# Three attention visits with float32 weights transposed by TensorE and divided by GpSimd, and values loaded once per batch

## The chip, the cores and the metric

One core of a Trainium2 chip runs the kernel. The time is that of one execution in device microseconds; the text names the engines PE (TensorE; PEld its weight loads), DVE (VectorE), ACT (ScalarE), POOL (GpSimd) and SP (SyncE, which issues nearly all DMAs here).

## The reference: what is computed

Attention in which a query sees only the keys of its own hash bucket, for 4 batches, 8 heads, 768 positions and 64 elements per head, and behind it a feed-forward layer with two weight matrices (512 to 2048 and back) and a squared ReLU, which the code calls MoE:

```python
q_bits = (np.einsum('bhsd,dk->bhsk', q, proj) > 0).astype(np.int64)
mask = q_bucket[:, :, :, None] == k_bucket[:, :, None, :]
scores = np.where(mask, scale * np.matmul(q, k.transpose(0, 1, 3, 2)), -1000000000.0)
attn = np.exp(scores - np.max(scores, axis=-1, keepdims=True))
attn = attn / (np.sum(attn, axis=-1, keepdims=True) + 1e-09)
x = np.matmul(attn, v).transpose(0, 2, 1, 3).reshape(B * S, H * D)
h = np.maximum(x @ w_in, 0.0)
return (h * h @ w_out).astype(np.float32)
```

All is float32, and the kernel keeps nearly that accuracy on fp16 matmuls: a number is split into an fp16 `hi` and an fp16 `lo` (what is left), and a product is made of three: hi by hi, hi by lo, lo by hi.

## The kernel before

**Visits and units.** The work is cut into visits: a batch, a pair of heads, and a half of the 768 queries (384). There are 32, and the first six are the pairs 0 and 1 of batch 0 with both halves, then pair 2 and pair 3 with half 0. A visit has six units (two heads by three blocks of 128 queries), so there are 192. One unit (`unit`, L651 to L673) does this:

- PE: scores `pS` of 128 queries by 768 keys; the mask is folded into the operands. In the first eight visits (batch 0) these are float32 matmuls over 128 rows, of which the trace shows two passes each; later ones are in a float32 form that takes less.
- DVE: `nmx`, the negated maximum of a row, read from PSUM.
- ACT: `e`, the exponential, with the row's sum `sm` beside it.
- POOL or DVE: `rv`, the sum scaled; DVE: its reciprocal.
- ACT (seldom POOL or DVE): the hi half `hl[:, 0] = e * rv` in fp16; DVE: the lo half, one instruction that reads `e` and the hi half.
- SP: one DMA transpose of both halves into `aT` (128 x 12 x 128, fp16).

When the six units of a visit have their `aT`, `av` (L679 to L686) multiplies them by the values: 36 matmuls in 18 pairs, the two heads of a pair side by side in the array, into `pA`. ACT and DVE split that again into `xx`.

**Values.** For each batch `scale_values` (L619) loads all four pairs of v, squares them (ACT), sums the squares of each row (DVE, `rows`) and takes the maximum, from which the power of two comes that v is scaled with. `values` (L638) then loads each pair once more and splits it into `VV`.

**MoE.** When the four pairs of a half are there, a stage of the MoE can start, of 112 steps with three matmuls each: `pm` (by w_in), ReLU and square and split on ACT and DVE (`g`), and `po` (by w_out). There are eight stages; the first needs the visits 0, 2, 4 and 5. During the first visits w_in and w_out are loaded too (`raw`, `f`) and split into fp16 halves (`win`, `wo`); at the end of the first stage `wo` is rescaled (`align`).

**Order.** The functions only record operations. A planner (`order`, `forward`, `backward`) then places them on the engines by estimated durations, ready times and ranks, and where an operation may run on several engines (`move`, `square`) it also chooses the engine. `emit` writes the result out; each engine takes its instructions in this order. A rule ties the MoE's steps to the units (`PACE`): step 0 not ahead of unit 25, step 120 not ahead of unit 64. And `emit` puts fillers in front of PE's instructions where the planner sees PE idle: matmuls of a tile of ones, without use for the result, into the PSUM tile with the tag `pm`, and only up to the first operation that needs a `pm` tile (`busy_from`):

```python
for i in out[: out.index(self.busy_from)]:
    ...
        if o.start > end + 300:
            fill[i] = int((o.start - end) * IDLE_SHARE / 56)
```

Line numbers: everything that is recorded comes out at L402, pairs and fours of matmuls at L399, fillers at L395; so the profile is read by tiles, not by lines. PSUM's eight banks are the tags `pS` (2), `po` (3, also used for the scores of every second unit up to unit 36), `pm`, `pA` and `misc` (1 each).

Of the kernel before, what the change touches and what calls it, by code (L numbers as in the profile page):

```python
# [40 lines left out]
ROUNDS, BEHIND = 4, 40000  # L41

PREP, STACKS, VALUES = -9, 0, 2
WIN_RANK, WOUT_RANK = (18, 2.0), (30, 2.5)
RANK_PE, RANK_MOE = 1e6, -1.0

PLAIN, ALTERNATE = 4, 36

WHOLE = {0: 2}
# [14 lines left out]

SWITCH = 95

# [46 lines left out]
class Program:  # L113
# [60 lines left out]
    def cost(key, name, args, kw):  # L174
# [10 lines left out]
        n = max(size(args[0]), size(args[1]) if isinstance(args[1], View) else 0)  # L185
        if key == "pe":
            t = max(107, size(args[2]) * column.get(args[2].dtype, 1 / 2.4) + 3)
            return t, t
        if name.startswith("dma"):
            b = int(np.prod(args[0].shape)) * mybir.dt.size(args[0].dtype)  # L190
            inside = name == "dma_start_transpose" or kinds[:2] == ["sb", "sb"]
            busy = 1040 if key == "pool" else (650 if inside else 475) + 50 * (key == "act")
            return busy, b / (175 if name == "dma_start_transpose" else 314)
        if key == "act":
# [9 lines left out]
    @staticmethod  # L204
    def tiling(o):

        _, w, x = (o.args[0][0] if o.name == "matmuls" else o.args)[:3]
        size = lambda n: min(m for m in (32, 64, 128) if n <= m)
        return size(w.shape[0]), 128 if w.dtype == F32R else size(int(np.prod(w.shape[1:])))

# [84 lines left out]
    def forward(self, prio, near):  # L295
# [20 lines left out]
        while True:  # L316
# [37 lines left out]
            if k == "pe":  # L354
                last, kind = kind, self.tiling(o)
                if last != kind:
                    busy, done = busy + SWITCH, done + SWITCH
            o.start, o.busy = t, busy
            if o.name.startswith("dma"):
# [55 lines left out]
def lsh_attention_moe(ctx: ExitStack, tc, kq, v, proj2, w_in, w_out, consts, out):  # L415
# [195 lines left out]

    vscales = {}

    def load(b, hp):
        RV = sb([P, 2, KC, D], F32, "RV")
        send(RV, v[b, hp])
        return RV

    def scale_values(b):  # L619

        tops = sb([P, H // 2], F32, "vtop", 2)
# [16 lines left out]
    def values(b, hp):  # L638
# [11 lines left out]

    def unit(st, half, i, aT):  # L651
        c0 = half * HS + i * P
# [14 lines left out]
        rv = sb([P, 1], F32, "rv", 3)  # L667
        pr.add(*[(q, "tensor_scalar", (rv, sm, 1e-9, 1.0 / ASC, ALU.add, ALU.mult), {}) for q in (dve, pool)])
        dve.reciprocal(rv, rv)
        hl = sb([P, 2, S], F16, "hl", BUFS["hl"])  # L670
        move(hl[:, 0], e, rv)
# [7 lines left out]
    def av(b, hp, half, VV, aTs):  # L679
        pA = ps([P, 512], F32, "pA")[:, 0:HS]  # L680
        todo = [(kc, t * D, kc + l * KC) for t, l in ((0, 0), (1, 0), (0, 1)) for kc in range(KC)]
        for n, (kc, d0, c) in enumerate(todo):
            matmuls(*[(pA[m], VV[:, h, kc, d0 : d0 + D], aTs[h][:, c]) for h, m in enumerate((T, U))], start=n == 0, stop=n == len(todo) - 1)
        xx = xxs[b, half, hp] = sb([P, 2, HS], F16, "xx")
        move(xx[:, 0], pA, 1.0 / ASC)
        left(xx[:, 1], pA, 1.0 / ASC, xx[:, 0])  # L686

# [115 lines left out]
    for n, (b, hp, half) in enumerate(visits):  # L803
        sts, aTs = kept[b, hp], []
        for h, st in enumerate(sts):
            aT = sb([P, 2 * KC, HS], F16, "aT", BUFS["aT"])
            aTs.append(aT)
            for i in range(3):
                pr.rank = u
                unit(st, half, i, aT)  # L810
# [3 lines left out]
        if (b, hp) not in kept_v or not alive([kept_v[b, hp]]):  # L814
            pr.rank = u - 6 + PREP
            kept_v[b, hp] = values(b, hp)
        pr.rank = u - 0.5
        av(b, hp, half, kept_v[b, hp], aTs)
        if n in early:
# [41 lines left out]
```

## Time and profile before

| | |
|---|---|
| median of 3 runs | 924.09 us (924.06 to 924.19) |
| the profiled execution | 925.36 us, its span 923.6 us |
| PE busy | 885.6 us (96%) |
| DVE busy | 643.8 us (70%) |
| ACT busy | 663.6 us (72%) |
| POOL busy | 54.8 us (6%) |
| DMA | 149.99 MB, mean 162 GB/s |

A row of a group reads: line, engine, operation, output tile <- input tiles, shapes, count | busy us in all, mean ns of one | idle us of the engine just before them, and what ended it. A row of a window: the stretch, its length, busy time (and count) of each engine, the clock that PE was granted (1.00 is full), the DMA engines' busy share, GB/s. A row of a timeline: start, duration, engine, operation, count, and the idle time before it. Records of one engine overlap a little, so that the distance of two starts is what an instruction holds of its engine.

### The profile page before, as it was taken

The numbers are of one execution on the slowest core, as the hardware profiler recorded it, in microseconds if no ns is written. First come the engines' busy times: TensorE is split into PE (matmuls) and PEld (weight loads), VectorE is DVE, ScalarE is ACT, GpSimd is POOL, SyncE is SP. The second block draws the span as 40 slices with busy tenths as digits, with TensorE's granted clock in tenths as the row PEclk, the third lists the DMA queues.
The fourth block names the chain that finished last, engine by engine and source line by source line (L and its number), as shares of the span: only waits on it lengthen the run. The fifth ranks groups of instructions, "written<-read, shape, count | busy, mean of one in ns | idle before, by whom it ended". The sixth has DMA issues, their size and how long they took to land.

```text
span 923.6 us, 15264 instructions
## 1 busy us (share of the span) xinstructions
PE 885.6 (96%) x5592; PEld 501.3 (54%) x5592; DVE 643.8 (70%) x1206; ACT 663.6 (72%) x1166; POOL 54.8 (6%) x104
## 2 busy tenths in 40 slices
PE   7988988999997999999999999999999999999997
PEld 6555555445554555555555556555555555554553
DVE  5999999988979687889686768797867651211111
ACT  4877987878879677888777768787778673533433
POOL 0111301200103000000000000000000000000000
PEclk9999999999999999999999999999999999999999
DMA  7998999997999797999697959897878640200000
GB/s 236 248 222 210 226 237 213 250 211 193 236 203 242 133 192 148 185 234 244 145 198 159 190 121 198 174 213 154 170 149 177 121 102 10 77 1 0 35 1 35
DMA packets 329323, 149.99 MB, mean 162 GB/s; under 512 B 305568, under 2 KB 305696, under 8 KB 329248
## 3 DMA queue, kind: packets, MB, share of 16 engines
q1 hardware_dynamic: 329248, 149.02, 73.6%
q8 instruction: 44, 0.72, 0.3%
q14 instruction: 31, 0.25, 0.1%
HBM read 43.59 MB, written 6.29 MB: 54 GB/s over the span
## 4 chain that ended last, share of the span: by engine, by line
PE 63%; ACT 5%; DMA 2%; DVE 2%; issue 1%; POOL 0%; SPq 0%; ACTq 0%; DVEq 0%
PE po L402 23%; PE pm L402 21%; PE pS L402 9%; PE pA L399 8%; ACT wo L402 1%; DMA aT<-hl 1%; ACT e L402 1%; PE pd L399 1%; DMA RV<-vp 1%; ACT hl L402 1%; DVE hl L402 1%; ACT g L402 1%; PE pc L402 1%; DVE nmx L402 1%; DMA M<-Q 1%
## 5 line engine op out<-in xcount | busy, mean ns | idle before, releaser
L402 PE MATMUL po<-wo,g 128*128 128x512 f16 x1152 | 332.7, 381 | 2.7 <-ACT wo L402 0.9
L402 PE MATMUL pm<-xx,win 128*128 128x384 f16 x1536 | 322.4, 327 | 1.3 <-DVE g L402 1.0
L402 DVE TENSOR_REDUCE nmx<-pS 128x1 f32<-128x768 f32 x192 | 183.1, 954 | 57.7 <-PE pS L402 56.6
L402 ACT ACTIVATE e<-pS,nmx 128x768 f32<-128x768 f32 x192 | 171.6, 894 | 67.8 <-DVE nmx L402 48.8
L402 DVE SCALAR_TENSOR_TENSOR hl<-e,rv,hl 128x768 f16<-128x768 f32 x192 | 194.1, 1012 | 26.1 <-ACT hl L402 25.5
L402 PEld LDWEIGHTS <-win 128*128 128x128 f16 x1536 | 145.1, 98 | 115.4 <-issue 17.8
L402 ACT ACTIVATE hl<-e,rv 128x768 f16<-128x768 f32 x188 | 173.5, 928 | 25.1 <-ACT e L402 14.0
L402 PEld LDWEIGHTS <-g 128*128 128x128 f16 x1152 | 107.9, 98 | 131.3 <-issue 26.4
L402 DVE SCALAR_TENSOR_TENSOR g<-g,g 128x384 f16<-128x384 f32 x122 | 67.5, 554 | 127.7 <-ACT g L402 127.1
L402 ACT ACTIVATE g<-pm 128x384 f32<-128x384 f32 x125 | 60.7, 486 | 108.3 <-PE pm L402 107.4
L402 ACT ACTIVATE g<-g 128x384 f32<-128x384 f32 (+1 forms) x248 | 128.8, 520 | 10.8 <-PE po L402 5.6
L399 PE MATMUL pA<-aT,VV 128*64 128x384 f16 x1152 | 117.8, 331 | 0.0
L402 PE MATMUL pS<-A,Q 128*128 128x384 f32 x288 | 95.2, 411 | 5.0 <-ACT e L402 4.8
L399 PEld LDWEIGHTS <-VV 128*64 128x64 f16 x1152 | 59.5, 109 | 55.8 <-issue 35.8
L402 PE MATMUL pS<-L,M 128*128 128x384 f32 x288 | 77.8, 350 | 0.2
L402 PEld LDWEIGHTS pS<-A,Q 128*128 128x128 f32 x288 | 49.3, 190 | 29.8 <-ACT e L402 15.9
L402 POOL TENSOR_SCALAR rv<-sm 128x1 f32<-128x1 f32 x74 | 28.8, 389 | 610.6 <-ACT e L402 604.0
L395 PEld LDWEIGHTS <-ones 128*128 128x128 bf16 x756 | 49.9, 103 | 20.1 <-issue 11.8
L395 PE MATMUL idle<-ones 128*128 128x128 bf16 x756 | 54.7, 228 | 2.7 <-DVE ones L402 2.7
L402 PEld LDWEIGHTS pS<-L,M 128*128 128x128 f32 x288 | 51.9, 189 | 3.9 <-issue 2.4
L402 PE MATMUL pS<-Q,M 128*128 128x384 f32 x96 | 37.3, 510 | 9.5 <-ACT e L402 9.1
L402 PE MATMUL pS<-A,L 128*128 128x384 f32 x96 | 36.6, 508 | 5.7 <-ACT e L402 5.4
(92 smaller groups left out, 579.9 us busy)
## 6 DMA issues: line engine op xcount, KB each, us to landing
RV<-vp SPq DMA_DIRECT2D x32, 384.0 KB
R<-kq SPq DMA_DIRECT2D x24, 384.0 KB
raw<-w_in SPq DMA_DIRECT2D x16, 511.8 KB
raw<-w_out SPq DMA_DIRECT2D x16, 511.8 KB
out<-o SPq DMA_DIRECT2D x21, 256.0 KB
Q<-L SPq DMA_DIRECT2D x24, 192.0 KB
Q<-A SPq DMA_DIRECT2D x24, 192.0 KB
L<-M SPq DMA_DIRECT2D x24, 192.0 KB
```

The costliest lines, as they stand in the source:

```text
L395: issue(q, q.engine.matmul(self.idle[0].real(), self.idle[1].real(), self.idle[1].real(), start=True, stop=True).ins)
L399: ins = q.engine.matmul(*map(real, args), **kw).ins
L402: ins = getattr(q.engine, o.name)(*map(real, o.args), **{k: real(x) for k, x in o.kw.items()}).ins
```

## The change

Three of the first five visits (`PLAIN_AV`: 0, 2 and 4, all of batch 0, 18 units) get another path from `e` to `aT`. POOL alone divides: it multiplies `e` by `rv` in place, in float32. PE transposes each of the six 128 x 128 blocks, three into a bank with the tag `pm` and three into one with the tag `pA`. ACT or DVE copies each of the two banks into `aT`, which is float32 in these visits. `hl` and the DMA transpose go. The values of these visits are the loaded float32 tile, unscaled, so `av` has 12 matmuls, in 6 pairs, instead of 36; the scale of v comes in when `pA` is split.

Values: the tile loaded for the scale is kept and used for the split (or, in the plain visits, as it is); 16 loads instead of 32. The square is one ACT instruction that writes the sum too; DVE's `rows` and `vtop` go. `unit_f`, the identity, gets a buffer of its own, and `VV` has six buffers, which v shares.

The planner's prices change a little (lines of `SWITCH`, `TRANSPOSES`), and with the operations everything is placed anew. The fillers end ahead of the first transpose now, since that is the first that needs a `pm` tile (`pr.busy_from` in `unit`).

```diff
-BUFS = dict(xx=12, hl=3, raw=2, f=7, e=3, aT=3, g=2, A=2, Q=2, L=2, M=2, RV=2, VV=4)
+BUFS = dict(xx=12, hl=3, raw=2, f=7, e=3, aT=3, g=2, A=2, Q=2, L=2, M=2, RV=2, VV=6)
...
+PLAIN_AV, DIVIDE = (0, 2, 4), ("pool",)
...
-SWITCH = 95
+SWITCH, ENTRY = 95, 105
+TRANSPOSES = 165
...
-    unit_f = sb([P, P], F32, "unit_f", tag="o")
+    unit_f = sb([P, P], F32, "unit_f")
...
         for hp in range(H // 2):
-            RV = load(b, hp)
-            rows = sb([P, 2 * KC], F32, "rows", 2)
-            square(RV, RV)
-            dve.tensor_reduce(rows, RV.rearrange("p h c d -> p (h c) d"), AX.X, ALU.add)
-            dve.tensor_reduce(tops[:, hp : hp + 1], rows, AX.X, ALU.max)
+            pr.rank = r0 + LOADS * hp
+            RV = loaded[b, hp] = sb([P, 2, KC, D], F32, "V", tag="VV")
+            send(RV, v[b, hp])
+            act.activation(sb([P, 2, KC, D], BF16, "sqv"), RV, AF.Square, accum_out=tops[:, hp : hp + 1])
...
-        RV = load(b, hp)
+        if plain:
+            return loaded[b, hp]
+        RV = loaded.pop((b, hp))
         VV = sb([P, 2, KC, 2 * D], F16, "VV")
...
+        if plain:
+            move(e, e, rv, tuple(getattr(pr, k) for k in DIVIDE))
+            for g in range(2):
+                pT = ps([P, 512], F32, "pT", tag=("pm", "pA")[g])[:, 0:HS]
+                pr.busy_from = min(pr.busy_from, len(pr.ops))
+                for c in range(3):
+                    kc = 3 * g + c
+                    pe.matmul(pT[:, c * P : (c + 1) * P], e[:, kc * P : (kc + 1) * P], unit_f, start=True, stop=True, is_transpose=True)
+                move(aT[:, 3 * g : 3 * g + 3, i * P : (i + 1) * P], pT.rearrange("p (c s) -> p c s", c=3), 1.0, (act, dve))
+            return
...
-        todo = [(kc, t * D, kc + l * KC) for t, l in ((0, 0), (1, 0), (0, 1)) for kc in range(KC)]
+        plain = VV.dtype == F32
+        todo = [(kc, t * D, kc + l * KC) for t, l in (((0, 0),) if plain else ((0, 0), (1, 0), (0, 1))) for kc in range(KC)]
+        scale = vscales[b][0] if plain else 1.0 / ASC
...
-            aT = sb([P, 2 * KC, HS], F16, "aT", BUFS["aT"])
+            aT = sb([P, KC, HS], F32, "aT") if plain else sb([P, 2 * KC, HS], F16, "aT")
```

How it moves the instructions is seen at three places. First DVE in the first units, from the second pair of score maxima on (`rv` is the reciprocal chain, `f` and `top` belong to w_in, `tov` and `norm` to the scale of v). Before:

```order
L402 TENSOR_REDUCE nmx<-pS 128x1
L402 SCALAR_TENSOR_TENSOR hl<-e,rv,hl 128x768
L402 TENSOR_SCALAR top_73<-raw 128x512
L402 SCALAR_TENSOR_TENSOR hl<-e,rv,hl 128x768
L402 SCALAR_TENSOR_TENSOR f<-raw,top_73 128x512
L402 TENSOR_REDUCE nmx<-pS_358 128x1
L402 RECIPROCAL rv<-rv 128x1
```

And now:

```order
L410 TENSOR_REDUCE nmx<-pS 128x1
L410 RECIPROCAL rv<-rv 128x1
L410 SCALAR_TENSOR_TENSOR f<-raw,top_79 128x512
L410 TENSOR_REDUCE norm<-pt 128x1
L410 TENSOR_REDUCE nmx<-pS_329 128x1
L410 TENSOR_SCALAR rv<-sm 128x1
```

The two hl between a maximum and the next are gone. Up to the sixth visit's xx DVE has 41 hl before and 22 now, 4 `rows` and none, 26 conversions to win and wo and 22, 43 maxima and 42, and one copy `aT<-pT`; ACT has 41 hl before and 22 now, and 35 copies `aT<-pT`.

Second PE at the same place (`pt<-dg,ones` belongs to the scale of v). Before, with fillers of L395 on both sides:

```order
L395 MATMUL idle<-ones 128x128
L402 MATMUL pS<-A,L 128x384 x2
L402 MATMUL pS_358<-Q,M 128x384 x2
L402 LDWEIGHTS ones
L402 MATMUL pt<-dg,ones 128x128
L395 LDWEIGHTS ones
```

And now:

```order
L410 MATMUL pS<-A,L 128x384 x2
L410 MATMUL pT<-unit_f,e 128x128 x3
L410 MATMUL pS_329<-Q,M 128x384
L410 LDWEIGHTS ones
L410 MATMUL pt<-dg,ones 128x128
L410 MATMUL pS_329<-Q,M 128x384
L410 MATMUL pT<-unit_f,e 128x128 x3
```

The transposes stand between the scores of later units, and no filler comes behind the first of them: 756 fillers before, 130 now. Ahead of the first `pm` PE has 88 score matmuls before and 86 now.

Third SP at the start (`cst`, `pj`, `sgn_f` and `unit_f` are constants; `A`, `Q`, `R` hold k and q). Before:

```order
L402 DMA Q<-kq 128x768
L402 DMA RV<-vp 128x768 x2
L402 DMA cst<-consts 128x4
L402 DMA pj<-proj 128x6 x2
L402 DMA sgn_f<-consts 6x64 x8
L402 DMA raw<-w_in 128x2047
L402 DMA R<-kq 64x768
```

And now:

```order
L410 DMA pj<-proj 128x6 x2
L410 DMA Q<-kq 128x768
L410 DMA sgn_f<-consts 6x64 x8
L410 DMA cst<-consts 128x4
L410 DMA R<-kq 64x768
L410 DMA V<-vp 128x768 x2
L410 DMA raw<-w_in 128x2047
```

The constants and the first R stand ahead of v now. Over the whole kernel SP has 192 transposes before and 174 now, and 32 loads of v and 16.

More of the change, by code (lines that the diff above doesn't have):

```diff
@@ L41 @@
 ROUNDS, BEHIND = 4, 40000
+LOADS = 0
 PREP, STACKS, VALUES = -9, 0, 2
@@ L186, in cost @@
         if key == "pe":
+            if "is_transpose" in kw:
+                return 110, 110
             t = max(107, size(args[2]) * column.get(args[2].dtype, 1 / 2.4) + 3)
@@ L192, in cost @@
             busy = 1040 if key == "pool" else (650 if inside else 475) + 50 * (key == "act")
-            return busy, b / (175 if name == "dma_start_transpose" else 314)
+            return busy, b / (TRANSPOSES if name == "dma_start_transpose" else 314)
         if key == "act":
@@ L355, in forward @@
                 last, kind = kind, self.tiling(o)
-                if last != kind:
+                if last is None or last[:2] != kind[:2]:
                     busy, done = busy + SWITCH, done + SWITCH
+                elif kind[2] and not last[2]:
+                    busy, done = busy + ENTRY, done + ENTRY
             o.start, o.busy = t, busy
@@ L610, in prep @@
         return out
[L612 to L617, printed above, removed]
+    vscales, loaded = {}, {}
     def scale_values(b):
+        r0 = pr.rank
         tops = sb([P, H // 2], F32, "vtop", 2)
         for hp in range(H // 2):
-            RV = load(b, hp)
-            rows = sb([P, 2 * KC], F32, "rows", 2)
-            square(RV, RV)
-            dve.tensor_reduce(rows, RV.rearrange("p h c d -> p (h c) d"), AX.X, ALU.add)
-            dve.tensor_reduce(tops[:, hp : hp + 1], rows, AX.X, ALU.max)
+            pr.rank = r0 + LOADS * hp
+            RV = loaded[b, hp] = sb([P, 2, KC, D], F32, "V", tag="VV")
+            send(RV, v[b, hp])
+            act.activation(sb([P, 2, KC, D], BF16, "sqv"), RV, AF.Square, accum_out=tops[:, hp : hp + 1])
         top = sb([P, 1], F32, "top")
@@ L636, in scale_values, with values @@
         vscales[b] = scales(norm, "v", 4)
-    def values(b, hp):
+        pr.rank = r0
+    def values(b, hp, plain):
         r0 = pr.rank
@@ L648, in values, with unit @@
         return VV
-    def unit(st, half, i, aT):
+    def unit(st, half, i, aT, plain):
         c0 = half * HS + i * P
@@ L667, in unit @@
         rv = sb([P, 1], F32, "rv", 3)
-        pr.add(*[(q, "tensor_scalar", (rv, sm, 1e-9, 1.0 / ASC, ALU.add, ALU.mult), {}) for q in (dve, pool)])
+        pr.add(*[(q, "tensor_scalar", (rv, sm, 1e-9, 1.0 if plain else 1.0 / ASC, ALU.add, ALU.mult), {}) for q in (dve, pool)])
         dve.reciprocal(rv, rv)
+        if plain:
[8 more added lines that the diff above has]
+            return
         hl = sb([P, 2, S], F16, "hl", BUFS["hl"])
@@ L684, in av @@
         xx = xxs[b, half, hp] = sb([P, 2, HS], F16, "xx")
-        move(xx[:, 0], pA, 1.0 / ASC)
-        left(xx[:, 1], pA, 1.0 / ASC, xx[:, 0])
+        move(xx[:, 0], pA, scale)
+        left(xx[:, 1], pA, scale, xx[:, 0])
     def unscaled(b, j=None):
@@ L803, in lsh_attention_moe @@
     for n, (b, hp, half) in enumerate(visits):
-        sts, aTs = kept[b, hp], []
+        sts, aTs, plain = kept[b, hp], [], n in PLAIN_AV
         for h, st in enumerate(sts):
-            aT = sb([P, 2 * KC, HS], F16, "aT", BUFS["aT"])
+            aT = sb([P, KC, HS], F32, "aT") if plain else sb([P, 2 * KC, HS], F16, "aT")
             aTs.append(aT)
@@ L809, in lsh_attention_moe @@
                 pr.rank = u
-                unit(st, half, i, aT)
+                unit(st, half, i, aT, plain)
                 u += 1
@@ L813, in lsh_attention_moe @@
             ready(*visits[n + 1][:2], u + PREP, visits[n + 1][0] == 0 and visits[n + 1][1] < PLAIN)
-        if (b, hp) not in kept_v or not alive([kept_v[b, hp]]):
+        if (b, hp, plain) not in kept_v or not alive([kept_v[b, hp, plain]]):
             pr.rank = u - 6 + PREP
-            kept_v[b, hp] = values(b, hp)
+            kept_v[b, hp, plain] = values(b, hp, plain)
         pr.rank = u - 0.5
-        av(b, hp, half, kept_v[b, hp], aTs)
+        av(b, hp, half, kept_v[b, hp, plain], aTs)
         if n in early:
```

2 lines of the change are left out of this document (1 added, 1 removed).

## The prediction

> **What bounds the kernel now.** I read the windows of busy time first, split where the profile changes character; the columns are PE, PEld, DVE, ACT and POOL busy, the granted clock, DMA share and GB/s.
>
> ```profile
> 0.00:20.00 20.00, 14.62 (x143) 12.46 (x144) 9.14 (x20) 7.68 (x10) 0.20 (x4) 0.91 0.74 220
> 20.00:170.00 150.00, 132.51 (x1087) 83.02 (x1086) 143.70 (x287) 120.77 (x202) 24.64 (x43) 1.00 1.01 228
> 170.00:200.00 30.00, 28.39 (x160) 14.32 (x159) 29.15 (x58) 27.03 (x49) 4.05 (x6) 1.00 0.98 231
> 200.00:272.00 72.00, 70.72 (x434) 39.48 (x433) 61.38 (x119) 58.69 (x105) 5.22 (x12) 1.00 0.96 217
> 272.00:298.00 26.00, 21.32 (x130) 12.24 (x129) 25.48 (x47) 25.09 (x33) 8.81 (x12) 1.00 0.98 223
> 298.00:924.00 626.00, 618.02 (x3646) 339.83 (x3644) 375.01 (x680) 424.32 (x770) 11.84 (x27) 1.00 0.63 133
> ```
>
> From 298 us on PE is busy 618 of 626 us: the end is PE's. Before 170 us it looks busy as well (132.5 of 150), but the groups of that stretch say with what:
>
> ```profile
> L395 PE MATMUL idle<-ones 128*128 128x128 bf16 x631 | 42.9, 219 | 0.0
> L402 DVE TENSOR_REDUCE nmx<-pS 128x1 f32<-128x768 f32 x44 | 41.8, 952 | 2.3 <-PE pS L402 2.2
> L402 DVE SCALAR_TENSOR_TENSOR hl<-e,rv,hl 128x768 f16<-128x768 f32 x41 | 41.5, 1011 | 0.8 <-ACT hl L402 0.8
> L402 ACT ACTIVATE e<-pS,nmx 128x768 f32<-128x768 f32 x43 | 38.4, 894 | 21.7 <-DVE hl L402 9.7 <-DVE nmx L402 5.5 <-DVE rv L402 4.5
> L402 ACT ACTIVATE hl<-e,rv 128x768 f16<-128x768 f32 x41 | 37.4, 925 | 0.1
> L402 PE MATMUL pS<-Q,M 128*128 128x384 f32 x84 | 32.8, 511 | 9.0 <-ACT e L402 8.6
> L399 PE MATMUL pA<-aT,VV 128*64 128x384 f16 x216 | 19.8, 329 | 0.0
> ```
>
> 42.9 us of it are filler matmuls that nobody reads, so PE does 89.6 us of work in 150. DVE is busy 143.7 (96%) and hardly ever waits (2.3 us for scores, 0.8 for hl), DMA's share is 1.01, ACT has 120.8 (81%). So two things are full at once: DVE by its own instructions, DMA by its transposes and loads. The stretch ends with the first matmul of the MoE:
>
> ```profile
> 169.50 1.30 PE L402 MATMUL pm<-xx,win 128*128 128x384 f16 x7
> ```
>
> From there PE has real work to put into every gap: of the 754 us that are left it is busy 738.4 (the sum of the last four windows), and some 15 us are lost. So the time is 169.5 us up to the first MoE matmul (T1 below), plus 754 us that are PE's. The change touches units of the visits 0, 2 and 4, all ahead of T1. What it is worth is how much earlier T1 comes, less what is given back behind it.
>
> **The change part by part.** Counts are from the orders of the two kernels, taken on each engine up to the sixth visit's xx, which is what the first MoE matmul waits for.
>
> *DVE.* Of hl's second halves 41 stand there before and 22 after: 18 belong to the plain units, one has moved behind T1. What one holds of the engine is the distance of starts:
>
> ```profile
> 106.65 1.01 DVE L402 SCALAR_TENSOR_TENSOR hl<-e,rv,hl 128x768 f16<-128x768 f32 x1
> 107.58 0.95 DVE L402 TENSOR_REDUCE nmx<-pS 128x1 f32<-128x768 f32 x1
> 108.44 0.15 DVE L402 RECIPROCAL rv<-rv 128x1 f32<-128x1 f32 x1
> ```
>
> 0.93 us each, so 18 x 0.93 = 16.7 us gone. The sums of squares of v go too (four `rows` of batch 0 and their maxima), but two of the four stood ahead of 19 us, where DVE was idle half the time; the other two at 0.95 count, 2 us with their small maxima. Only one of the 36 copies of transposed weights falls to DVE, +0.5. Net 18.2 us. Besides, five conversions of w_in (three at 0.69, two shorter), a score maximum and that hl stand behind T1 now, about 4.9 us. DVE ahead of T1: 143.7 - 23.1 = 120.6 us.
>
> ```profile
> L402 DVE TENSOR_REDUCE rows<-RV 128x12 f32<-128x768 f32 x16 | 15.0, 945 | 6.7 <-ACT RV L402 6.6
> L402 DVE TENSOR_SCALAR g<-pm 128x384 f32<-128x384 f32 x3 | 1.7, 553 | 0.2 <-PE pm L402 0.2
> L402 ACT ACTIVATE xx<-pA 128x384 f16<-128x384 f32 x31 | 15.0, 483 | 16.1 <-PE pA L399 15.7
> L402 POOL TENSOR_SCALAR hl<-e,rv 128x768 f16<-128x768 f32 x3 | 2.9, 954 | 0.6 <-DVE rv L402 0.6
> L402 DVE SCALAR_TENSOR_TENSOR f<-raw,top 128x512 uint32<-128x512 uint32 x27 | 18.7, 697 | 0.0
> L402 DVE SCALAR_TENSOR_TENSOR win<-f,towin,win 128x512 f16<-128x512 f32 x16 | 12.0, 770 | 0.8 <-POOL win L402 0.8
> L402 POOL TENSOR_SCALAR rv<-sm 128x1 f32<-128x1 f32 x30 | 11.7, 389 | 113.0 <-ACT e L402 109.7 <-DVE hl L402 3.4
> ```
>
> *ACT* trades 19 hl at 0.925 (17.6 us) for 35 copies out of PSUM, nearest row xx<-pA at 0.483 (16.9 us); the squares of v keep their place and gain an accumulator read each. It comes out even: 121 us.
>
> *POOL* gets 18 divisions of 128x768; the nearest row is its three hl at 0.954, so 17 us, on an engine with 24.6 of 150 busy. Its own time is free, but it disturbs: its 128x1 scaling takes 0.389 us in the mean, most of it behind DVE's long instructions with two inputs from SBUF (hl, f, win). If such a pair excludes each other, each division that meets one holds DVE back by half its length. Those instructions fill about 60 of DVE's 121 us (22 hl and 4 of v at 0.93, 26 f at 0.70, 22 of the weights at 0.77 or less); 18 x 0.5 x 0.48 = 4 us. Bounds: 0 (DVE goes first always) and 17.
>
> *PE* loses the fillers, and three visits of 36 fp16 matmuls in pairs (19.8 / 2 = 9.9 us); it gets 36 float32 ones in pairs, each in two passes as pS has them, and 108 transposes.
>
> ```profile
> 26.38 1.56 PE L402 MATMUL pS<-Q,M 128*128 128x384 f32 x4 [0.23 <-ACT e L402]
> 27.77 1.11 PE L395 MATMUL idle<-ones 128*128 128x128 bf16 x17
> ```
>
> Four float32 passes over 384 columns take 1.56 us, 0.39 each, so a pair of value matmuls is 0.78 and three visits 18 x 0.78 = 14 us. No float32 transpose is in this trace. Below lies the filler, 128 columns at 1.11 / 17 = 0.065 us (7 us in all), above two passes of a pS at 0.39 / 3 each beside a weight load of 0.19 (41 us in all); I take one pass of 128 float32 columns, 0.13, 14 us. PE's work is 89.6 - 9.9 + 14 + 14 = 108 us, 101 to 135.
>
> The Trainium skill (VectorE: DVE Perf Modes, section on the three transpose paths) gives 390 ns for a 128x128 bf16 transpose on TensorE. By that figure, as an estimate, the transposes would be 42 us and PE's work 136. No run here shows it yet.
>
> *DMA* loses 18 transposes of the 36 of this stretch and four loads of v; its share was 1.01, so it drops out as a bound. And its order at the start changes: the small constants stand ahead of v now. Before, DVE's cast of the signs stood idle 2.9 us for a load:
>
> ```profile
> 12.86 0.43 DVE L402 CAST sgn<-sgn_f 128x512 bf16<-128x512 f32 x1 [2.89 <-DMA raw<-w_in]
> 18.30 2.80 PE L402 MATMUL pS<-A,L 128*128 128x384 f32 x8
> ```
>
> I let the first scores come 3 us earlier (0 to 4).
>
> *T1.* With the start at 17 instead of 20: DVE needs (120.6 + 4) / 0.96 = 130 us, the 0.96 being what it reached before. ACT needs 121 us of its own; the most that it reached before T1 in any 20 us was 18.31:
>
> ```profile
> 40.00:60.00 20.00, 18.08 (x137) 11.12 (x135) 19.90 (x39) 18.31 (x32) 3.19 (x9) 1.00 0.97 218
> ```
>
> At 0.92 that is 131 us. PE's 108 us fit in. So T1 = 17 + 131 = 148 us, 21.5 earlier, with DVE and ACT as bounds side by side.
>
> *Behind T1.* The 4.9 us of DVE work that has moved lands in a stretch like 170 to 200, where DVE is full (29.15 of 30): I give back half, 2.5 us. In 272 to 298, where PE loses 4.7 us, ACT rescales w_out:
>
> ```profile
> L402 ACT ACTIVATE wo<-wo,rel 128x1024 f16<-128x1024 f16 x15 | 16.2, 1138 | 0.0
> L402 DVE TENSOR_SCALAR wo<-wo,rel 128x1024 f16<-128x1024 f16 x1 | 0.5, 466 | 0.0
> ```
>
> The order has 9 of these on ACT now, 6 on DVE and 1 on POOL: I count 2 us of the 4.7 as won. The loads and squares of v in the batches 1 to 3 go in a stretch that is PE's: nothing.
>
> *The clock.* Without fillers PE has gaps. The rows (PE alone: busy, clock, DMA) of the two places in the trace where that happened:
>
> ```profile
> 9.00:12.00 3.00, 1.84 (x25) 1.00 0.54 131
> 12.00:15.00 3.00, 1.50 (x18) 0.94 0.99 287
> 15.00:18.00 3.00, 3.00 (x27) 0.50 1.01 283
> 18.00:21.00 3.00, 3.00 (x17) 0.99 1.05 378
> ...
> 294.00:298.00 4.00, 2.08 (x11) 1.00 1.02 219
> 298.00:302.00 4.00, 4.00 (x13) 0.58 1.06 271
> ```
>
> A stretch with PE half idle costs half the clock for the three or four us behind it; 61% busy did not yet. At 108 of 131 us (82%) I expect a few such dips, like the one in 272 to 302: about 4% of PE's work, 4 us, of which 3 on the path.
>
> Sum: -21.5 + 2.5 - 2 + 3 = -18 us. The profiled execution took 925.36 us (span 923.6), the median of the runs is 924.09, 1.3 less; the difference is carried over to the median: 906.1 us.
>
> **The rivals.**
>
> 1. *The hand-offs eat it.* A plain unit goes ACT e, reciprocal, POOL, PE, ACT, each engine taking its instructions in order, with three buffers for e and one bank for each half of pT. For it: ACT's idle time ahead of e is 21.7 us already, all behind DVE. Against it: ACT, the receiver, has other work in between. If each of 18 units holds ACT up by 0.5 us more, 9 us: 915.
>
> 2. *More than I count.* ACT and DVE both wait less when DMA is no longer full: ACT at 0.97 makes T1 142, and all of the 4.7 us behind are won; without clock loss that is -27.5 - 4.7 + 2.5, near -30: 894. Against it: ACT has never run so full ahead of T1.
>
> 3. *Slower, by the clock.* If the granted clock stays down through the stretch, PE is the bound: from 17 us on it has 108 us to do, and at a mean clock c takes 108 / c. Even with before is c = 108 / 152.5 = 0.71; at 0.6 T1 comes at 197, 27.5 us late: 952. For it: the fillers go, and 0.50 and 0.58 stand in the rows above. Against it: those dips end after some 3 us of work, and a PE that falls behind is busy, which brought 0.99 each time. The Trainium skill (TensorE: Matmul & The Clock Gate, Part 4 on the PE-mode transpose) says that transposes do not count as busy for the clock gate as matmuls do. By that rule 94 of 131 us count instead of 108, 72%, still over the 61% that kept the clock here; it gets 6% from me.
>
> 4. *Nothing comes of it*, because the MoE's steps are tied to units and w_in's last chunks come later: 924. DVE's total work up to 298 us falls by about 20 us whatever the order, so this gets 2%.
>
> **How the numbers follow.** The forecast has 0.62, with ends at 897 and 915: port 0 instead of 4, start 4 and all of the 4.7 below; POOL's upper bound or a transpose at its upper end above (PE at 135 of 131 us makes T1 155 or so). Rival 1 has 0.20, rival 2 has 0.10, rival 3 0.06, rival 4 0.02. 893 to 919 leaves out rival 3 and 4 and some of the tails. What can be told from no change here is 0.2%, 1.8 us: faster 0.92, same 0.02, slower 0.06.
>
> **What would show it.** In the profile after: the first pm at 144 to 152 us; DVE and ACT both above 90% between 20 us and there; DMA's share at 0.8; no filler behind the first transpose; POOL's division near 0.95; the transposes' distance near 0.13; the clock mostly at 1.00 with dips. A first pm at 160 with ACT waiting for pT says rival 1; a clock of 0.7 or less over the stretch says rival 3. An early T1 with an end that has not moved would make the forecast wrong where I trust it most: that behind T1 the time is PE's.

## The result, and the profile after

The kernel after takes 914.86 us (median of 4 runs, 912.07 to 916.78), the kernel before 924.14 beside it (4 runs): a ratio of 0.988, interval 0.9847 to 0.9913. So it is faster, by 9.3 us where the forecast had 18. The profiled execution took 913.5 us with a span of 911.7; before it was 925.36 and 923.6. A second measurement is the first experiment below; it gave 11.3 us. In three of the sets below (the loading of v alone, a price of 175, the two that helped together) one run took 1261 to 2259 us; the ratios leave it out, and the medians change by at most 0.15 us with it.

The windows of the kernel after, cut at its own first MoE matmul (153.5 us) and then as before:

```profile
0.00:20.00 20.00, 15.28 (x142) 11.66 (x143) 7.37 (x16) 8.60 (x14) 0.20 (x4) 0.92 0.74 231
20.00:153.50 133.50, 112.09 (x525) 56.77 (x524) 121.62 (x253) 115.25 (x216) 43.06 (x62) 0.95 0.79 192
153.50:200.00 46.50, 44.99 (x261) 23.48 (x260) 41.66 (x84) 42.51 (x79) 7.79 (x11) 1.00 1.02 218
...
272.00:298.00 26.00, 25.48 (x147) 13.88 (x148) 19.09 (x34) 21.17 (x38) 0.33 (x1) 1.00 1.05 200
298.00:912.00 614.00, 604.01 (x3558) 328.04 (x3556) 360.91 (x650) 413.21 (x754) 17.75 (x31) 1.00 0.65 128
```

Ahead of T1 DMA's share is 0.79 instead of 1.01, POOL has 43 us instead of 24.6, and DVE is busy 91% where it was 96%. In 272 to 298, where w_out is rescaled, PE is busy 25.48 us instead of 21.32.

The groups between 20 us and T1:

```profile
L410 DVE TENSOR_REDUCE nmx<-pS 128x1 f32<-128x768 f32 x41 | 38.9, 952 | 9.0 <-PE pS L410 8.8
L410 ACT ACTIVATE e<-pS,nmx 128x768 f32<-128x768 f32 x42 | 38.1, 909 | 7.2 <-DVE nmx L410 4.7 <-DVE rv L410 1.7 <-POOL rv L410 0.3
L410 PE MATMUL pS<-A,L 128*128 128x384 f32 x80 | 33.8, 545 | 7.3 <-ACT e L410 4.5 <-ACT L L410 2.8
L410 PE MATMUL pS<-Q,M 128*128 128x384 f32 x84 | 33.7, 519 | 7.8 <-ACT e L410 7.7
L410 DVE SCALAR_TENSOR_TENSOR hl<-e,rv,hl 128x768 f16<-128x768 f32 x22 | 22.4, 1019 | 0.2
L410 POOL TENSOR_SCALAR e<-e,rv 128x768 f32<-128x768 f32 x18 | 18.8, 1048 | 38.3 <-DVE rv L410 28.5 <-PE pS L410 3.3 <-PE pc L410 2.3
L410 PE MATMUL pT<-unit_f,e 128*128 128x128 f32 x108 | 17.2, 277 | 1.8 <-ACT aT L410 1.2 <-POOL e L410 0.6
L410 ACT ACTIVATE aT<-pT 128x384 f32<-128x384 f32 x35 | 16.5, 502 | 1.1 <-PE pT L410 0.9
L407 PE MATMUL pA<-aT,V 128*64 128x384 f32 x72 | 12.9, 494 | 0.0
```

Of hl on DVE 22 are left, POOL divides 18 times, ACT copies 35 times: the counts of the order. What is new is in the last column: DVE waits 9.0 us for scores (2.3 before). ACT waits 7.2 us ahead of its exponential, 21.7 before. The scores wait 12.2 us for that exponential (7.7 and 4.5); this is not new, since before it was 13.7 (8.6 for `Q,M`, and 5.1 in this row of the stretch from 20 to 170 us), with fillers in a part of the gaps:

```profile
L402 PE MATMUL pS<-A,L 128*128 128x384 f32 x88 | 33.7, 508 | 5.4 <-ACT e L402 5.1 <-ACT L L402 0.3
```

The timeline of PE, at the first scores, at six transposes in a row, at the first float32 value matmuls, and at T1:

```profile
15.52 2.96 PE L410 MATMUL pS<-A,L 128*128 128x384 f32 x6 [2.07 <-ACT L L410]
...
25.96 0.82 PE L410 MATMUL pT<-unit_f,e 128*128 128x128 f32 x6
26.61 0.81 PE L410 MATMUL pS<-Q,M 128*128 128x384 f32 x2
...
39.28 1.19 PE L407 MATMUL pA<-aT,V 128*64 128x384 f32 x6
...
153.53 1.79 PE L410 MATMUL pm<-xx,win 128*128 128x384 f16 x10
```

T1 came at 153.53 instead of 169.50, 16.0 us earlier. Behind it the kernel takes 758.2 us and not 754.1.

**How far PE is at 300 us.** A first matmul is one point; how much work is left at a fixed time is a better measure. The groups of PE from 300 us on, before and after:

```profile
L402 PE MATMUL po<-wo,g 128*128 128x512 f16 x1004 | 294.9, 381 | 0.8 <-ACT o L402 0.8
L402 PE MATMUL pm<-xx,win 128*128 128x384 f16 x1296 | 277.2, 326 | 0.1
L399 PE MATMUL pA<-aT,VV 128*64 128x384 f16 x756 | 80.7, 332 | 0.0
L402 PE MATMUL pS<-A,Q 128*128 128x384 f32 x238 | 79.1, 412 | 1.4 <-ACT e L402 1.4
L402 PE MATMUL pS<-L,M 128*128 128x384 f32 x238 | 64.7, 352 | 0.0
```

```profile
L410 PE MATMUL po<-wo,g 128*128 128x512 f16 x963 | 287.2, 380 | 1.6 <-ACT o L410 0.8 <-DVE g L410 0.4 <-ACT g L410 0.2
L410 PE MATMUL pm<-xx,win 128*128 128x384 f16 x1264 | 272.7, 326 | 1.0 <-ACT g L410 0.7
L407 PE MATMUL pA<-aT,VV 128*64 128x384 f16 x744 | 80.3, 333 | 0.0
L410 PE MATMUL pS<-A,Q 128*128 128x384 f32 x230 | 74.8, 405 | 0.0
L410 PE MATMUL pS<-L,M 128*128 128x384 f32 x230 | 61.9, 348 | 1.3 <-DMA M<-Q 1.3
```

The kernel after has 41 `po`, 32 `pm`, 12 `pA` and 16 `pS` less to do. By their distances of starts between 300 and 750 us (0.216, 0.163, 0.0725 and 0.22 us) that is 8.9 + 5.2 + 0.9 + 3.5 = 18.5 us of lead. The spans differ by 11.9. So 6.6 us are lost again behind 300 us, where by the forecast nothing was left to lose. That is what the experiments had to explain. Below, "lead" is this count at 300 us against the kernel before, and "lost" is the lead less the difference of the spans.

### The profile page after: what moved, and what is told of

It is laid out like the page before. It is cut to its first block, busy times and chain, and to the rows that moved or that the text cites. A ratio compares the mean times of both kernels' runs of the same rounds, so it can differ in the third digit from the quotient of the medians.

```text
span 911.7 us, 14110 instructions
## 1 busy us (share of the span) xinstructions
PE 871.3 (96%) x5038; PEld 472.1 (52%) x5038; DVE 614.6 (67%) x1150; ACT 664.4 (73%) x1208; POOL 75.7 (8%) x120
## 5 line engine op out<-in xcount | busy, mean ns | idle before, releaser
L410 PEld LDWEIGHTS <-win 128*128 128x128 f16 x1536 | 145.7, 98 | 116.1 <-issue 18.1
L410 DVE SCALAR_TENSOR_TENSOR hl<-e,rv,hl 128x768 f16<-128x768 f32 x174 | 176.3, 1015 | 27.8 <-ACT hl L410 27.0
L410 ACT ACTIVATE hl<-e,rv 128x768 f16<-128x768 f32 x174 | 161.7, 931 | 23.8 <-ACT e L410 16.7
L410 ACT ACTIVATE g<-g 128x384 f32<-128x384 f32 (+1 forms) x252 | 131.2, 521 | 6.8 <-PE po L410 1.8
L407 PE MATMUL pA<-aT,VV 128*64 128x384 f16 x1044 | 110.0, 333 | 0.0
L407 PEld LDWEIGHTS <-VV 128*64 128x64 f16 x1044 | 53.9, 109 | 54.0 <-issue 37.2
L410 POOL TENSOR_SCALAR rv<-sm 128x1 f32<-128x1 f32 x77 | 37.3, 485 | 511.2 <-ACT e L410 477.6
L410 PE MATMUL pS<-A,L 128*128 128x384 f32 x96 | 41.0, 553 | 9.8 <-ACT L L410 4.9
L410 DVE TENSOR_SCALAR M<-pc,cst 128x384 fp32r<-128x384 f32 (+1 forms) x56 | 37.6, 671 | 3.9 <-PE pc L410 3.9
L410 ACT ACTIVATION_READ_ACCUMULATOR e<-pS,nmx 128x1 f32 x192 | 38.1, 198 | 0.0
```

The costliest lines, as they stand in the source:

```text
L407: ins = q.engine.matmul(*map(real, args), **kw).ins
L410: ins = getattr(q.engine, o.name)(*map(real, o.args), **{k: real(x) for k, x in o.kw.items()}).ins
```

## The experiments

Two questions were put: what holds T1 (the clock or the hand-offs), and what takes the lead away behind 300 us. The first four kernels ran on one chip beside the kernel before, each ratio is to that; so did the next four, and the three after them.

**1. The kernel after once more.**

> The changed kernel as it is, on the chip of the next three. Its four runs lay between 912.1 and 916.8 us, with mean granted clocks of 0.987 to 0.992, where the kernel before stayed within 924.1 to 926.4. Theory K (the clock): the missing fillers leave PE at half clock for a few short stretches, their number differs from run to run, and so does the time; 912 to 917 again, median near 914.5, a lower clock with every longer run. Theory H (the hand-offs between ACT, POOL and PE in a plain unit are what limits, the clock only goes with it): the same times, but no order between clock and time.

Measured: 913.3 us (912.08 to 913.86), ratio 0.9879, interval 0.9866 to 0.9892; T1 153.7, lead 17.4, lost 5.8. What follows: the gain is 11 us with a spread of about 2 between sets, and lead and loss are nearly the same in a second execution. Between the theories this set does not decide: the clocks of its runs, from the shortest to the longest, are 0.996, 0.988, 0.992 and 0.987.

**2. Fillers up to the first MoE matmul.** The transposes no longer end the fillers, and these write to a spare quarter of a bank: 410 of them instead of 130, the same plan.

```diff
-                issue(q, q.engine.matmul(self.idle[0].real(), self.idle[1].real(), self.idle[1].real(), start=True, stop=True).ins)
+                spare = [x for x in self.idle[0].rec.line if x.tile is not None]
+                spare = spare[-1].tile[:, 384:512] if spare else self.idle[0].real()
+                issue(q, q.engine.matmul(spare, self.idle[1].real(), self.idle[1].real(), start=True, stop=True).ins)
...
-                pr.busy_from = min(pr.busy_from, len(pr.ops))
```

> The same plan with fillers all the way to the first MoE matmul, written into the unused 128 columns of the bank that pT uses; nothing else differs. Theory K: the three half-clock stretches between 88 and 147 us (13.6 us long in all, some 5 us of PE's work in them lost) go; first pm at 148 to 151 instead of 153.5, time 909 to 911, and the runs agree within 1 us. Theory H: the clock goes up, but the first pm stays at 152 to 155 and the time at 913 to 916.

Measured: 911.08 us (910.72 to 911.75), ratio 0.9858, interval 0.9845 to 0.9871. T1 150.8, and the window from 20 us to there:

```profile
20.00:150.80 130.80, 120.75 (x798) 72.15 (x801) 121.45 (x253) 114.16 (x214) 41.94 (x62) 1.00 0.83 196
```

What follows: the clock is at 1.00 instead of 0.95, T1 comes 2.9 us earlier, and 2.2 us of it arrive at the end (913.3 to 911.08). That is Theory K, at the upper end of its ranges. The rows of the kernel after show where the clock went, PE alone:

```profile
85.00:88.00 3.00, 1.32 (x8) 1.00 1.01 260
88.00:95.50 7.50, 5.73 (x15) 0.54 1.16 225
...
130.00:133.00 3.00, 0.81 (x3) 0.98 1.04 189
132.50:136.50 4.00, 3.30 (x5) 0.57 1.03 283
...
140.00:143.00 3.00, 0.63 (x2) 1.00 0.92 235
143.00:147.00 4.00, 4.00 (x18) 0.57 0.87 210
```

Ahead of each dip stand 3 us with PE busy 21% to 44%. None of the three lies where transposes run: these start in 22.3 to 35.9, 54.3 to 76.4 and 99.9 to 116.2 us, and there the clock held. What costs the clock is that the fillers are gone in the other stretches too.

**3. No division.** The same plan without POOL's 18 divisions; the weights of the plain visits stay undivided, so this part of the computation is left out.

```diff
+            if i in self.skip:
+                continue
...
+            pr.skip.add(len(pr.ops))
             move(e, e, rv, tuple(getattr(pr, k) for k in DIVIDE))
```

> The same plan without the 18 divisions on POOL: the weights of the plain visits stay undivided, and each transpose waits for ACT's exponential alone. Theory H: a hand-off and 18.8 us of POOL's time, some of it excluding DVE's long instructions, go; hl, f and VV on DVE come back to their lengths of before, first pm 3 to 6 us earlier, time 908 to 911. Theory K: POOL is off the path in this order, 1 us at most: 913 to 916.

Measured: 911.79 us (910.7 to 920.45), ratio 0.9889, interval 0.9857 to 0.992; T1 151.1. What follows: by the medians 1.5 us less than 913.3, and its interval holds that of the kernel after. The time lies between the ranges of the two theories, and DVE's hl did not get shorter (1.025 us in the mean, 1.019 with the divisions). Nor need all of the 2.4 us at T1 be the division's: the mean clock from 20 us to T1 is 0.97 in this execution and 0.95 in that of the kernel after. The way over POOL costs little; of rival 1 there is no more than this in these units.

**4. The loading of v alone.** `PLAIN_AV = ()`: no plain visit, but v loaded once, squared on ACT, and the new prices.

> The other half of the change alone: no plain visit, but values loaded once and squared on ACT with the sum beside it; planned anew, fillers as before. By my sum for the whole change this part holds the earlier start (3 us), two of DVE's four row sums of batch 0 (2 us) and four loads of 384 KB in a stretch where DMA is full: 918 to 921 if it is that. A rival says that the loads are the larger part, since DMA's share was 1.01: 4 of them there at about 1.5 us each beside the start, 914 to 917, nearly all that the change brings. And if DVE alone counts, 921 to 924.

Measured: 927.35 us (926.04 to 928.11), ratio 1.0027, interval 1.0014 to 1.0041. T1 159.3, which is 10 us earlier than before, and yet the end is later. Lead at 300 us 7.1, lost 9.0. No theory had that. What follows: T1 is no measure of its own, since the planner may put the first MoE step ahead of units (42 units' scores stood ahead of it, 44 before); and 9 us can go behind 300 us without a plain visit.

**5. The plain visits alone.** v is loaded twice and squared on DVE as before, and `VV` has four buffers again; the rest as after.

```diff
-            RV = loaded[b, hp] = sb([P, 2, KC, D], F32, "V", tag="VV")
-            send(RV, v[b, hp])
-            act.activation(sb([P, 2, KC, D], BF16, "sqv"), RV, AF.Square, accum_out=tops[:, hp : hp + 1])
+            RV = load(b, hp)
+            rows = sb([P, 2 * KC], F32, "rows", 2)
+            square(RV, RV)
+            dve.tensor_reduce(rows, RV.rearrange("p h c d -> p (h c) d"), AX.X, ALU.add)
+            dve.tensor_reduce(tops[:, hp : hp + 1], rows, AX.X, ALU.max)
```

> Three plain visits, but v is loaded twice per batch and squared on DVE as before (the loading part of the change is undone). Theory A (the two parts add up): the loading part alone took 2.8 us more than the kernel before (927.35 against 924.57), so without it the gain is 11.3 + 2.8 = 14 us: 910 to 911. Theory I (they work together: the loading part takes 2 us of sums of squares from DVE and four loads from DMA, and lets the first scores come 3 us earlier, which is of use only when DVE and DMA are relieved by the plain visits): the first scores at 18.3 instead of 15.5, some 3 to 5 us lost: 916 to 918.

Measured: 913.44 us (909.93 to 915.3), ratio 0.9864, interval 0.9843 to 0.9885; T1 152.8, lead 11.6, lost 1.5. It lies between the two theories and decides for neither: the lead is 6 us smaller than that of the kernel after, and so is the loss nearly. The plain visits carry the whole gain; whether v's part adds a lead that the order then loses stays open, since the order is another one here.

**6. and 7. Only another order.** The kernel before with the planner's price of a DMA transpose of the kernel after, and the kernel after with that of before. The work is the same in each pair; with the order the planner also moves some small operations to another engine.

```diff
-            return busy, b / (175 if name == "dma_start_transpose" else 314)
+            return busy, b / (165 if name == "dma_start_transpose" else 314)
```

> The kernel before, with nothing changed but the planner's price of a DMA transpose (165 bytes a nanosecond instead of 175, as in the kernel after): the same work in another order. It sizes what a new order alone does to the time. Theory N (order matters by several us, so that the 6 us which the kernel after loses behind 300 us need no cause of their own): time 2 to 5 us away from 924.6 on either side, and PE's lost time behind 300 us, 7.6 in the kernel before, anywhere in 6 to 14. Theory S (the loss belongs to the change): time within 1 us of 924.6, lost time behind 300 us within 1 of 7.6.

Measured: 927.5 us (926.08 to 928.88), ratio 1.0026, interval 1.0016 to 1.0037; T1 166.8, lead -1.5, lost -0.2 against the kernel before. The time, 2.6 us more, speaks for Theory N, the lost time for Theory S. (The lost time of the expectations has PE's idle time of the kernel before behind 300 us in it, 7.6 us; "lost" here is without these.)

> The kernel after, with nothing changed but the planner's price of a DMA transpose (175 bytes a nanosecond instead of 165, as in the kernel before). Theory N (order alone is worth several us): 2 to 5 us away from 913.3 on either side, PE's lost time behind 300 us anywhere in 6 to 14. Theory S (the loss belongs to the change): within 1 us of 913.3, lost time behind 300 us near 13.4.

Measured: 923.74 us (919.86 to 926.0), ratio 0.9979, interval 0.9965 to 0.9994; T1 145.1, lead 15.8, lost 13.1. Theory S falls, and Theory N had the effect too small. One number of the planner takes 10 of the 11 us away, although T1 comes 8 us earlier still. PE has the same matmuls in both but for the fillers (123 instead of 130); of the 174 hi halves on ACT two go to POOL and one to DVE, and some small operations change engines likewise. So it is the plan that differs, and not the work.

**8. Five plain visits.** `PLAIN_AV = (0, 1, 2, 3, 4)`.

> All first five visits plain instead of three. Theory L (the gain is a count of relieved DVE instructions): two visits more are 12 of hl's second halves less on DVE, 11 us, and by the rate of the three (11.3 us measured) 7 us: 905 to 907. Theory B (another engine is full by then): ACT trades even and was at 89% in the kernel after, PE gets 2 x (3.3 + 4.7) us more and GpSimd 12 divisions; the gain of the last two is 0 to 2 us or negative: 911 to 916, with DMA's share ahead of the first MoE matmul below 0.6.

Measured: 911.45 us (910.78 to 915.04), ratio 0.9859, interval 0.9839 to 0.9879; T1 150.4, lead 21.0, lost 10.7. The window from 20 us to T1:

```profile
20.00:150.40 130.40, 117.14 (x574) 62.74 (x575) 111.01 (x242) 116.39 (x229) 50.53 (x66) 0.97 0.64 168
```

DMA's share ahead of T1 is 0.64, not below 0.6; DVE is at 85% and ACT at 89%. Two plain visits more bring 3 us of lead: Theory B, by the time. By the profiled execution 4 us more are lost than in the kernel after, but that one took 915.04 us, 3.6 over the median; in it PE waits 1.89 us, up to 387.5 us, for the DMA that fills `M`, and the clock is at 0.50 in 388.0 to 391.4.

**9. to 11. More orders of the kernel after.** A price of 160 and of 170 for a DMA transpose, and no price (0 instead of 105) on PE's step into a float32 matmul, which undoes one line of the change.

> The kernel after with the planner's price of a DMA transpose at 160 bytes a nanosecond instead of 165; the same work in another order. At 175 it took 923.7, at 165 913.3. Theory P (the price is right at 165, and the time grows with the distance from it): about 918, between the two, by PE's lost time behind 300 us. Theory N (any other order of the same work lands somewhere in a band, without a trend): PE's lead at 300 us over the kernel before 12 to 21 us, its lost time behind 300 us 7 to 20, time anywhere in 909 to 924.

Measured: 923.09 us (920.71 to 925.07), ratio 0.9984, interval 0.9971 to 0.9997; T1 152.8, lead 9.3, lost 8.8. The time is in Theory N's band, the lead below it.

> The kernel after with the planner's price of a DMA transpose at 170 bytes a nanosecond, half way between 165 (913.3) and 175 (923.7). Theory P (a trend): 917 to 920. Theory N (a band without a trend): anywhere in 909 to 924, with the lost time behind 300 us deciding it, and with it the number of scores that start late behind a MoE matmul (over 0.15 us after it: 3 of 103 in the kernel before, 22 of 103 in the kernel after).

Measured: 916.47 us (915.5 to 920.73), ratio 0.992, interval 0.9901 to 0.994; T1 151.6, lead 14.4, lost 4.5. 18 of 100 scores start late. The time just misses Theory P's range, and 160 with 923 is far from it: there is no trend about 165.

```diff
-SWITCH, ENTRY = 95, 105
+SWITCH, ENTRY = 95, 0
```

> The kernel after without the new price of 105 ns that the planner puts on PE's step into a float32 matmul; the same work. Theory P (the price is part of the gain, since without it the planner takes PE to be ahead of where it is and scores come late): 3 to 6 us slower than 913.3, with more scores that start late than the 22 of 103. Theory N (it only shuffles the order): anywhere in 909 to 924, without relation to the price.

Measured: 907.25 us (905.07 to 908.85), ratio 0.9813, interval 0.9794 to 0.9833; T1 149.2, lead 21.0, lost 0.7. Theory P had the wrong sign: without the price the kernel is 6 us faster, below Theory N's band too, and 9 of 98 scores start late. Its groups of PE from 300 us on:

```profile
L410 PE MATMUL po<-wo,g 128*128 128x512 f16 x964 | 282.0, 381 | 0.8 <-ACT o L410 0.8
L410 PE MATMUL pm<-xx,win 128*128 128x384 f16 x1260 | 266.6, 327 | 0.2
L407 PE MATMUL pA<-aT,VV 128*64 128x384 f16 x720 | 77.1, 333 | 0.0
L410 PE MATMUL pS<-A,Q 128*128 128x384 f32 x230 | 76.3, 410 | 1.4 <-ACT e L410 1.3
L410 PE MATMUL pS<-L,M 128*128 128x384 f32 x231 | 60.9, 344 | 0.0
```

About as much is left to do as in the kernel after, but for 24 `pA`. The records of `po`, which overlap where they follow each other closely, cover 282.0 us instead of 287.2 for as many, and the wait for the DMA of `M` is gone.

**What is lost behind 300 us.** All orders beside each other. The last two columns compare distances of starts between 300 and 750 us with those of the kernel before: "late scores" is what the scores of a unit start later in all after the MoE matmul ahead of them, "around pA" is what the steps from the value matmuls to others and back cost more.

| | us | T1 | lead | lost | late scores | around pA |
|---|---|---|---|---|---|---|
| before | 924.6 | 169.5 | 0 | 0 | 0 | 0 |
| before, price 165 | 927.5 | 166.8 | -1.5 | -0.2 | 1.0 | 0.5 |
| after, no entry price | 907.25 | 149.2 | 21.0 | 0.7 | 0.9 | -1.1 |
| after (price 165) | 913.3 | 153.5 | 18.1 | 6.2 | 4.7 | 1.6 |
| after, price 170 | 916.5 | 151.6 | 14.4 | 4.5 | 4.1 | 2.3 |
| after, price 160 | 923.1 | 152.8 | 9.3 | 8.8 | 2.0 | 5.7 |
| after, price 175 | 923.7 | 145.1 | 15.8 | 13.1 | 7.0 | 7.5 |
| plain visits alone | 913.4 | 152.8 | 11.6 | 1.5 | 6.0 | -2.8 |
| loading of v alone | 927.35 | 159.3 | 7.1 | 9.0 | 5.2 | 3.1 |
| five plain visits | 911.45 | 150.4 | 21.0 | 10.7 | 5.6 | 5.7 |

(The table counts by starts from 300 us on; the rows of groups count what still runs at 300 too, so that the kernel after has a lead of 18.1 here and of 18.5 there. It also counts the `pd` matmuls, at 0.1 us each. The times are medians of several sets, in which the kernel before took 924.1 to 925.8.) Lead and lost come from one profiled execution each, which took 3.6 us more than the median with five plain visits, 1.9 more with the plain visits alone, 1.8 more with a price of 160, and 2.2 less without the entry price; such a difference stands in "lost". The sum of the last two columns is within 2 us of "lost" in every row. So the loss has two parts.

The leads differ too, and the table does not explain them. One thing that goes with them is the clock between 20 and 300 us: its mean is 0.98 in the kernel after and 0.95 with a price of 160. That is 30.7 us at half clock instead of 13.9, up to 8.4 us of PE's work, and the lead is 8.8 us smaller. No run here has that order with fillers, so this is not shown to be the cause; with a price of 170 the lead is 3.7 us smaller with 13.7 us at half clock.

First, late scores. The timeline of the kernel after shows one of them, on PE and ACT:

```profile
330.66 1.67 PE L410 MATMUL po<-wo,g 128*128 128x512 f16 x7
...
331.22 0.90 ACT L410 ACTIVATE e<-pS,nmx 128x768 f32<-128x768 f32 x1 [0.65 <-DVE nmx L410]
332.02 0.19 ACT L410 ACTIVATION_READ_ACCUMULATOR e<-pS,nmx 128x1 f32 x1
...
332.26 0.30 PEld L410 LDWEIGHTS pS<-A,Q 128*128 128x128 f32 x2 [0.42 <-ACT e L410]
332.26 0.62 PE L410 MATMUL pS<-A,Q 128*128 128x384 f32 x2
```

The scores start 0.05 us after ACT has read the sum of the unit ahead, whose exponential empties the bank; the weight load stood idle for that for 0.42 us. Here ACT itself had waited 0.65 us for DVE's maximum. In the kernel before 3 of 103 scores behind a MoE matmul start over 0.15 us after it, in the kernel after 22 of 103; 19 of these 22 have the end of ACT's `e` 0.05 us ahead of them. In 13 of the 19 ACT comes to the exponential straight from other work, in 5 it has waited for DVE's maximum, and in one, for 0.07 us, for DVE's reciprocal. The other three are the half `L,M`; for one the trace names the DMA that fills `M`, for two it names no wait. The row of the weight loads of these scores, 300 to 750 us, in the kernel before:

```profile
L402 PEld LDWEIGHTS pS<-A,Q 128*128 128x128 f32 x234 | 40.4, 190 | 19.4 <-ACT e L402 7.5 <-ACT g L402 2.3 <-issue 2.0
```

And after:

```profile
L410 PEld LDWEIGHTS pS<-A,Q 128*128 128x128 f32 x229 | 37.7, 189 | 22.6 <-ACT e L410 14.5 <-issue 1.9 <-ACT xx L410 0.6
```

Waiting for the exponential went from 7.5 to 14.5 us; a part of it lies beside matmuls that still run. ACT is no fuller in this stretch than it was (347 of 450 us busy, 349 before): the exponentials come at other times.

Second, the steps from and to the value matmuls, which use 64 columns of the array (128*64 in their rows) where the others use 128. The last value matmul ahead of a `po` holds PE 0.2 us longer than the 0.0725 of one among its kind, and a `po` ahead of a value matmul 0.1 us longer. The Trainium skill (TensorEngine Tiling (Array Packing), section Key Properties) says that a change of the tiling mode drains TensorE; the trace agrees, with 0.28 us in place of 0.07. PE leaves `pA` 81 times in the kernel before, 84 in the kernel after, 99 with a price of 160, 104 with 175 and 77 without the entry price. But the column "around pA" also holds scores that start late behind a value matmul: that step takes 0.264 us in the mean before, 0.353 with a price of 170 and 0.422 with five plain visits, which is nearly all of the 2.3 us of the one and 3.8 of the 5.7 of the other (there the half clock from 388.0 us on lies in it as well).

This is an account from the records. No kernel here kept the order and moved the exponentials alone, so that these two are the cause is argued, not shown; that the plan takes the lead away, and not the work, is shown by the kernels with the same work.

**12. The two that helped, together.**

> The two that helped, together: no price on the step into a float32 matmul (907.25 alone) and fillers up to the first MoE matmul (911.08 alone, 2.2 less than the kernel after). Theory A (the clock's loss and the order's loss are separate, and add up): 13.6 us of half clock ahead of the first MoE matmul go, T1 at 146 to 147 instead of 149.2, time 904.5 to 905.5. Theory O (in this order the clock's dips lie beside waits for DVE and ACT and cost nothing): T1 within 0.5 of 149.2, time 907 to 908.

Measured: 906.15 us (905.12 to 911.36), ratio 0.9798, interval 0.9772 to 0.9825; T1 148.3, lead 20.1, lost 1.0. What follows: the clock's dips ahead of T1 are gone, but only 0.9 us at T1 and about 1 in the time come of it: between the two theories, nearer to Theory O. Of the kernels here these two, with 906.15 and 907.25, are the fastest, and their intervals overlap.

## Why the prediction was right, and where not

**What bounds the kernel, and where the gain arises:** right as to the engine and the place. At 300 us the forecast had 21.5 less 3 for the clock, less 2.5, plus 2: 18 us. Measured: 18.5. That it is so close is luck in part, since two errors cancel: T1 came 16.0 us earlier and not 18.5, while between T1 and 298 us PE lost 4.6 us of 144.5, where the kernel before lost 7.6 of 128 from 170 us on. These are 3 us won in a stretch in which the forecast gave back 0.5.

**T1 = 148:** 153.5. DVE's work was right (121.6 us busy; 120.6 and up to 4 in the text), ACT's 115 and not 121. What failed is the step from work to time: DVE at 96% and ACT at 92%. They reached 91% and 86%, because the chain of a unit shows: scores, maximum, exponential, next scores. DVE waits 9.0 us for scores, and still 7.9 with fillers and the full clock; which link of the chain is to blame no run tells. Of the 5.5 us, 2.9 are the half clock (T1 150.8 with fillers), in which a unit's four scores take 2.92 us (at 133.16) instead of 1.56. The forecast had put 3 us for that in its sum, so it had the size, and not that they fall on T1.

**The prices.** Six transposes hold PE from 25.96 to 26.61: 0.108 us each (0.13 taken). By the 390 ns that the Trainium skill gives for a bf16 one (VectorE: DVE Perf Modes, section on the three transpose paths) these six would have taken 2.3 us; the trace has 0.65. The float32 value matmuls start 0.152 us apart, 72 of them make 10.9 us (14 taken); the mistake was to price them by scores. ACT's copy takes 0.502 (0.483 taken). POOL's division takes 1.048 us in the mean (0.954 taken), but there are two kinds: eleven of the 18 take 0.91 to 0.95, and seven 1.19 to 1.37, all seven beside a DVE instruction with two inputs from SBUF (six `f`, one `win`) that was already running. The other way round it happened once at length:

```profile
101.32 0.91 POOL L410 TENSOR_SCALAR e<-e,rv 128x768 f32<-128x768 f32 x1 [1.85 <-ACT e L410]
101.64 1.39 DVE L410 SCALAR_TENSOR_TENSOR VV<-V,tov,VV 128x768 f16<-128x768 f32 x1
...
103.44 0.69 DVE L410 SCALAR_TENSOR_TENSOR f<-raw,top 128x512 uint32<-128x512 uint32 x1
103.53 1.37 POOL L410 TENSOR_SCALAR e<-e,rv 128x768 f32<-128x768 f32 x1 [0.45 <-DVE rv L410]
```

The division that had begun first kept its 0.91 us, and `VV` took 1.39 where the other fifteen in this trace take 1.00 to 1.02; with five plain visits the same happened to a `win` (1.24 us instead of 0.73) and a `wo` (1.10). So the mechanism of the term is borne out, the two exclude each other, and its size was too high: the one that comes second waits, that was POOL in these seven cases, and DVE lost some 0.4 us and not 4. None of DVE's 22 hl stands beside a division.

**The start**, 3 us: 15.52 instead of 18.30, 2.8.

**The rescale of w_out**, 2 us won: PE's loss in 272 to 298 went from 4.7 to 0.5, though 2.3 us of idle time stand at 260 to 270 now, where there were none.

**Behind T1 all is PE's:** right as to the engine (604 of 614 us busy), and wrong in what was drawn from it, that a lead is kept. The term is missing from the sum: 6.6 us that are lost again behind 300 us. That the plan does it is shown; that it does so by late scores and changes of shape is the account above. The busy time hides it: a record of `po` is 0.38 us long where the starts are 0.216 apart, so that one that starts 0.16 late leaves no idle time.

**From the profile to the median:** the profiled execution was 1.3 us over the median before and 1.4 under it after, at 913.5; 2.7 us of the difference to 906.1 are that, and it is the spread of the runs: the second set of the same kernel has its median at 913.3. So the time is off by 8.8 us: 6.6 by the order, less 0.5 of lead more than forecast, and 2.7 by this.

**The rivals.** Rival 1 named hand-offs by way of POOL and 915 us. The time is there, the mechanism is not: without the division 1.5 us are gone, and ACT waits only 1.1 us for `pT`. Rival 2 had the rescale of w_out right (4.2 of the 4.7 us are won) and the rest not: ACT reached 86% and not 97%. A hand-off it seems to be, though, from ACT's exponential to the next scores, in units that the change does not touch. Rival 3 did not come: mean clock 0.95 ahead of T1. On the rule that transposes do not count as busy for the clock (TensorE: Matmul & The Clock Gate, Part 4 on the PE-mode transpose, in the Trainium skill) the traces do not decide: in the three stretches with transposes PE is busy 64% to 66% without them, and 61% had held the clock before. Rival 4 is excluded by the lead.

**How sure the sign was.** 0.92 for faster was too much for what the profile could say. The same work in five orders took 907 to 924 us; all five are faster than the kernel before by their intervals, but two by 0.16% and 0.21% only, and which order the planner would hit the profile could not say.

## What to carry to other kernels

Where a planner places the work, a change is work and order at once: time two or three orders of the same work (nudge one of the planner's numbers) before the difference is put down to the work. Measure progress by the work that is left at a fixed time, not by when the next stage starts, and look in the tail for what is given back, at the distances of starts rather than at the busy share. Fillers that end at an operation are lost in every stretch behind it, also in those without it.

## What the runs showed that was not expected

- Float32 transposes of 128 x 128 follow each other on PE every 0.108 us, with their weight loads beside them.
- A plan alone is worth 16 us here (907.25 to 923.7 for the same work), more than the change.
- A DVE instruction with two inputs from SBUF and POOL's 128 x 768 division exclude each other, and the second waits: the division takes 0.91 us or, behind `f` or `win`, 1.19 to 1.37; `VV` takes 1.0 us or, behind a division, 1.39.
- Half the clock comes in pieces of 3.4 us or a multiple of it; in the kernel after each one between 20 us and T1 stands behind some 3 us with PE busy 21% to 44%, and with five plain visits one comes in the tail, at 388 us, behind 3 us with PE busy 37%.
